# Loading two weight matrices in 32-row transfers, with a new order of the work

## The chip, the cores and the metric

One core of a Trainium2 chip runs the whole program. The metric is the device time of one execution in microseconds (us), median over several runs; less is better.

## The reference, cut to what matters

An RWKV-style recurrence over r, k, v of shape (4, 8, 768, 48) is followed by a feed-forward block on 3072 tokens of 384 columns:

```
cur = einsum('bhd,bhe->bhde', u * k_t, v_t)
y_t = einsum('bhd,bhde->bhe', r_t, state + cur)
state = w * state + einsum('bhd,bhe->bhde', k_t, v_t)
x = y as (3072, 384)
out = (((x @ w1) * (x @ w2)) @ w3) @ w_out
```

w1 and w2 are 384 x 1024, w3 is 1024 x 1024, w_out is 1024 x 384. These four arrive as 8-byte floats; everything is computed in 4-byte floats.

## The kernel before, in words

The sequence is cut into 24 units (six chunks of 128 steps for each of four batches). For a unit, k and r are scaled with tables of powers of w (`k`, line 432), turned so that head columns stand on partitions (`T`, `R` by PE for the first five units; `x`, `y`, `z`, `l` through a scratch in device memory for the others: VectorE turns blocks, SP writes them out and reads them back into the tile tt, ScalarE copies), multiplied (`U` line 551, `A` line 561, `S` line 670, `V` line 700), taken (`Y`), turned (`yt`) and put into xT (`yx`). Then come the products with w1 and w2 (`a`, `b`, line 748: full ones of 512 tokens, half ones of 256; for later chunks `pa`, `pb`, line 907, in halves of the width) and their elementwise product (`u`, `ga`, `gb`).

w3 and w_out don't depend on the tokens, so the kernel multiplies them once: w34 = w3 @ w_out, in eight folds (`F`, line 419, one for each block of 128 rows of w3; each needs all eight pieces of w_out, and its block of w3 turned by VectorE, `G`, line 412). The products with w34 are made by a scheme of seven products instead of eight (`s`, `P` line 807, `E`, `D`); those of `pa` and `pb` use the like for w1 and w2.

The weights come in 32 pieces (`W`, lines 233 to 244): eight strips of w1 and w2 (768 KB), eight pieces of w_out (384 KB), sixteen of w3 (512 KB; two for each fold). Each lands in one of three raw buffers, `raws[i % 3]`. The 8-byte floats are then made into 4-byte ones in five steps (lines 365 to 403): `M` magnitude (ScalarE), `p` sign (POOL, line 391; `N` is the same on VectorE, line 382), `H` high word (VectorE, line 395), `L` low word (ScalarE, line 398), `Q` total (VectorE, line 402). After `L` the raw buffer is free for the third piece on. The sign tile has two buffers.

At the start a table of powers is made (lines 281 to 306), turned by PE (line 311) and put into pn_in (line 313), with which k and r of the first units are scaled.

All engines but the two branches around it follow one list, ORDER (lines 23 to 104): each word is one step on its engine (`names`, line 957), each engine takes its instructions in the order of the list, and so do SP's transfers. A transfer that waits on SP holds all that come behind it. With 1425 words before and after, the list is where every step stands in its queue.

Of the kernel before, what the change touches and what calls it, by code (L numbers as in the profile page):

```python
# [28 lines left out]
V.3 Q.2 W.5 c.0.0.0 U.5 Y.3 H.4 ps p.3 v.6 M.3 cz.1 ub L.4 H.3 yt.3 W.7 b.0.0.0 Q.4 yx.3 L.3 k.7 a.0.2.2 W.6 Q.3 M.5
p.5 z.5 u.0.0.0 vs.6 u.0.1.0 H.5 a.0.4.2 c.0.2.2 e.5 L.5 f.5 Q.5 M.7 p.7 b.0.1.1 h.5 c.0.4.2 H.7 a.0.0.1 W.8 M.6 p.6  # L30
d.6 e.6 L.7 b.0.4.2 H.6 c.0.0.1 W.10 L.6 Q.7 Q.6 M.8 p.8 W.9 b.0.2.2 l.5 H.8 f.6 L.8 p.10 Q.8 M.10 W.11 H.10 b.0.5.2
u.0.2.2 M.9 p.9 u.0.4.2 L.10 H.9 W.13 Q.10 L.9 Q.9 a.0.1.1 M.11 p.11 W.12 d.7 H.11 kr.10 a.0.5.2 c.0.1.1 e.7 L.11 f.7
W.14 M.13 p.13 Q.11 H.13 M.12 p.12 u.0.1.1 b.0.3.2 L.13 H.12 c.0.5.2 W.16 Q.13 L.12 u.0.5.2 W.15 Q.12 a.0.6.2 M.14
p.14 d.8 e.8 H.14 L.14 p.16 M.16 Q.14 W.17 A.5 M.15 p.15 H.16 b.0.6.2 c.0.6.2 i.5 L.16 m.5 W.19 j.5 H.15 a.0.3.2 L.15
Q.16 M.17 Q.15 W.18 p.17 G.0.0 H.17 b.0.0.1 p.19 u.0.6.2 L.17 c.0.3.2 Q.17 W.20 a.0.7.2 G.0.1 M.18 p.18 u.0.3.2 M.19
u.0.0.1 H.18 F.0 H.19 L.18 L.19 Q.18 W.21 M.20 Q.19 p.20 W.22 c.0.7.2 G.1.0 G.1.1 H.20 L.20 p.21 M.21 Q.20 W.23 F.1
X.0 H.21 M.22 p.22 G.2.0 L.21 H.22 W.24 Q.21 L.22 Q.22 M.23 p.23 W.25 G.2.1 H.23 U.4 X.1 G.3.0 F.2 L.23 i.4 p.24 M.24
W.26 j.4 Q.23 M.25 G.3.1 p.25 k.6 x.6 kr.9 M.26 H.25 y.6 S.4 H.24 L.25 F.3 fe.4 L.24 Q.25 W.28 X.2 Q.24 p.26 G.4.0
W.27 H.26 G.4.1 L.26 x.7 z.6 Q.26 M.28 p.28 V.4 H.28 X.3 U.6 Y.4 v.7 p.27 S.5 cz.0 L.28 y.7 yt.4 fe.5 k.8 V.5 yx.4
W.29 F.4 M.27 Q.28 l.6 G.6.0 v.8 H.27 vs.7 Y.5 W.31 L.27 x.8 g.6 Q.27 z.7 p.29 M.29 f.8 P.0.0.0 H.29 X.4 vs.8 G.5.0  # L40
p.31 yt.5 y.8 L.29 A.6 G.5.1 W.30 yx.5 b.0.7.2 m.6 g.7 i.6 kr.11 j.6 Q.29 l.7 S.6 G.6.1 U.7 fe.6 z.8 u.0.7.2 A.7 M.30
p.30 V.6 m.7 M.31 F.6 i.7 j.7 v.9 H.30 Y.6 L.30 H.31 l.8 Q.30 G.7.0 L.31 s.0.1.0 vs.9 U.8 wa.0 A.8 X.6 wa.1 F.5 Q.31
G.7.1 wa.3 wb.0 wa.2 s.0.1.1 i.8 k.9 yt.6 X.5 F.7 wb.1 yx.6 g.8 wb.3 x.9 k.10 y.9 s.0.1.2 j.8 m.8 S.7 s.0.0.0 X.7 U.9
z.9 fe.7 B.0 V.7 P.0.1.0 Y.7 B.1 yt.7 v.10 E.0.1.0 s.0.0.1 pa.1.0.0 yx.7 xs.1.0 E.0.0.0 P.0.1.2 ga.1.0.0 xs.1.1 xs.1.2
xs.1.3 l.9 pb.1.0.4 B.3 pa.1.0.4 vs.10 x.10 pa.1.0.1 B.2 y.10 s.0.0.2 k.11 pa.1.0.5 ga.1.0.5 pb.1.0.0 s.0.1.3 ga.1.0.1
ga.1.0.3 pa.1.0.6 z.10 s.0.0.3 pa.1.0.7 ga.1.0.2 x.11 pa.1.0.3 ga.1.0.4 y.11 wb.2 d.9 pa.1.0.2 ga.1.0.7 e.9 kr.12
gb.1.0.0 f.9 d.10 g.9 pb.1.0.5 e.10 kr.13 f.10 pa.1.1.0 d.11 pb.1.0.1 e.11 gb.1.0.1 kr.14 f.11 ga.1.0.6 gb.1.0.3
pb.1.0.6 gb.1.0.5 pb.1.0.7 d.12 gb.1.0.2 e.12 pb.1.0.2 gb.1.0.4 gb.1.0.8 E.0.1.2 pb.1.0.3 gb.1.0.6 s.1.0.0 s.1.0.1 S.8
# [1035 lines left out]
```

## Time and profile before

| | |
|---|---|
| median of 3 runs | 564.42 us (563.61 to 565.67) |
| profiled execution | 559.54 us, span 557.8 us |
| busy | PE 493.7, PEld 402.7, VectorE (DVE) 328.5, ScalarE (ACT) 196.2, GpSimd (POOL) 64.9 us |
| moved by DMA | 52.72 MB, mean 95 GB/s |

PE is the matmul engine and PEld its weight loads. "SPq" is SyncE's queue, which issues the transfers. A matmul of 4-byte floats stands as two instructions in the trace, so a fold of eight matmuls is x16. "PEclk" is the granted clock as a share of the upper level. An engine's idle time matters only where others wait for it.

### The profile page before, as it was taken

Reading aid. Unit: us, or ns where it says so; the run is one execution under the profiler, and the core shown is the slowest. Engines: PE = TensorE matmul, PEld = TensorE weight load, DVE = VectorE, ACT = ScalarE, POOL = GpSimd, SP = SyncE. Lnnn points to the kernel's source line nnn. Section 1 sums busy time; section 2 is a strip of 40 time slices with the busy share of each in tenths; the row PEclk is TensorE's granted clock in tenths of the full one; section 3 lists DMA queues with packets and bytes.
Section 4 is the critical chain, followed back from the end, with each engine's and each line's share of the span. In section 5 each row is a group of like instructions: output and inputs, shape, how many; then the busy total and the mean of one; then the engine's idle time right before and its main releaser. Section 6 shows DMA issues by size and latency. Waiting matters only on the chain.

```text
span 557.8 us, 12087 instructions
## 1 busy us (share of the span) xinstructions
PE 493.7 (89%) x5084; PEld 402.7 (72%) x5084; DVE 328.5 (59%) x645; ACT 196.2 (35%) x450; POOL 64.9 (12%) x61
## 2 busy tenths in 40 slices
PE   7889674774547799999999999999999999999996
...
PEclk9989878687859799999999999999999999999999
DMA  8998232222344424403236326622220001000001
GB/s 183 224 242 241 103 101 100 100 97 101 122 140 146 115 72 117 98 15 114 59 106 138 86 73 176 153 58 86 72 86 29 29 28 43 31 31 0 1 0 63
DMA packets 99104, 52.72 MB, mean 95 GB/s; under 512 B 77920, under 2 KB 88416, under 8 KB 99040
## 3 DMA queue, kind: packets, MB, share of 16 engines
...
q8 instruction: 42, 0.69, 0.5%
...
q10 hardware_dynamic: 624, 0.00, 0.1%
...
## 4 chain that ended last, share of the span: by engine, by line
PE 66%; DMA 20%; DVE 4%; SPq 3%; ACT 3%; POOL 2%; issue 1%; ACTq 0%; POOLq 0%; DVEq 0%
DMA raw<-in_moe_w_dram 10%; PE ps_accB L917 9%; DMA raw<-in_moe_w_out_dram 5%; DMA tt<-scratch 5%; PE ps_Ab L917 3%; PE ps_accC L917 3%; PE ps_accC L921 3%; PE ps_accB L921 3%; PE ps_s4b L812 3%; PE ps_s3t L812 3%; PE ps_s1t L812 3%; PE ps_s2t L812 3%; PE ps_a22t L812 3%; PE ps_Aa L917 3%; PE ps_a12b L812 3%; PE ps_a11b L812 3%
## 5 line engine op out<-in xcount | busy, mean ns | idle before, releaser
L391 POOL TENSOR_SCALAR t<-raw 128x512 f32<-128x512 f32 (+2 forms) x32 | 54.5, 1705 | 121.1 <-DMA raw<-in_moe_w_dram 75.2
L422 PE MATMUL ps_w<-wo,w3T 128*128 128x384 f32 x128 | 48.9, 541 | 10.2 <-DVE w3T L417 10.2
L422 PEld LDWEIGHTS ps_w<-wo,w3T 128*128 128x128 f32 x128 | 26.6, 213 | 29.4 <-issue 12.9
L917 PE MATMUL ps_accB<-sumw,w 128*128 128x256 f32 x160 | 45.6, 387 | 0.0
L754 PE MATMUL ps_a<-xT,w 128*128 128x512 f32 (+1 forms) x60 | 29.8, 651 | 11.9 <-DVE abt L763 11.9
L396 DVE SCALAR_TENSOR_TENSOR w3n<-w3n,t 128x512 uint32<-128x512 uint32 x16 | 10.9, 691 | 44.4 <-POOL t L391 44.4
L466 ACT ACTIVATE ynat<-vnat,dg 128x48 f32<-128x48 f32 x144 | 34.4, 324 | 0.1
L522 ACT COPY kT<-tt 128x1024 f32<-128x1024 f32 x19 | 19.9, 1046 | 36.9 <-PE ps_y L685 31.8
L917 PEld LDWEIGHTS ps_accB<-sumw,w 128*128 128x128 f32 x160 | 28.9, 190 | 5.5 <-ACT u3a L934 1.1
L754 PEld LDWEIGHTS ps_a<-xT,w 128*128 128x128 f32 x60 | 13.8, 241 | 25.6 <-DVE abt L763 14.3
L754 PE MATMUL ps_b<-xT,w 128*128 128x512 f32 (+1 forms) x60 | 25.1, 567 | 7.9 <-ACT a L760 7.0
L400 ACT ACTIVATE t<-raw 128x512 uint32<-128x512 uint32 (+2 forms) x32 | 22.2, 701 | 22.9 <-DVE w3n L396 11.8
L436 DVE TENSOR_TENSOR krs<-krin,pn_in 128x768 f32<-128x768 f32 (+1 forms) x25 | 23.3, 937 | 9.5 <-PE ps_a L565 5.3
L380 ACT ACTIVATE w3n<-raw 128x512 f32<-128x512 f32 x16 | 10.4, 665 | 49.6 <-DMA raw<-in_moe_w_dram 49.6
L685 PE MATMUL ps_y<-st,kT 64*64 64x48 f32 x320 | 14.5, 226 | 13.0 <-ACT w L425 11.9
L754 PEld LDWEIGHTS ps_b<-xT,w 128*128 128x128 f32 x60 | 12.4, 217 | 18.1 <-ACT a L760 8.1
L685 PEld LDWEIGHTS ps_y<-st,kT 64*64 64x64 f32 x320 | 11.8, 138 | 18.4 <-ACT w L425 12.2
L917 PE MATMUL ps_accC<-xT,sumw 128*128 128x256 f32 x80 | 24.1, 383 | 0.1
L921 PE MATMUL ps_accB<-xT,w 128*128 128x256 f32 x80 | 23.8, 379 | 0.0
L921 PE MATMUL ps_accC<-xT,w 128*128 128x256 f32 x80 | 23.8, 379 | 0.0
L917 PE MATMUL ps_Ab<-xT,w 128*128 128x256 f32 x80 | 22.7, 385 | 0.3 <-DVE ynat L717 0.3
L730 ACT COPY xT<-ps_x 128x384 f32<-128x384 f32 x24 | 11.4, 482 | 32.0 <-PE ps_x L724 31.9
...
## 6 DMA issues: line engine op xcount, KB each, us to landing
...
```

The lines of the kernel that those rows point to most:

```text
L391: nc.gpsimd.tensor_scalar(part["t", i].bitcast(F32), words(i)[1].bitcast(F32), 0.0, None, ALU.mult)
L400: nc.scalar.activation(out=part["t", i], in_=words(i)[0], func=COPY, scale=2.0 ** -29)
L422: nc.tensor.matmul(ps, lhsT=w3T[j][:, kc, :], rhs=wo[kc], start=(kc == 0), stop=(kc == KF - 1))
L436: nc.vector.tensor_mul(krs[n % NS][:, which, :, :D], kr[:, which], pn[:, which, :, :D])
L466: nc.scalar.activation(out=ynat[n][:, h, :], in_=vnat[n % NV][:, h, :], func=COPY, scale=dg[n][:, h:h + 1])
L522: nc.scalar.copy(out=turned(n).rearrange("x g p (z t) -> x (g p) z t", t=Q), in_=tts.rearrange("x z e t -> x e z t"))
L685: nc.tensor.matmul(yt[n][i][rows(a), p, :], lhsT=rw[rows(i), p, rows(a)], rhs=(half[n % 2] if a else st[b][(c + 1) % 2])[rows(i), p, :], s ...
L730: nc.scalar.copy(out=xT[c][:, :, b * C:(b + 1) * C], in_=pst["y", n])
L754: nc.tensor.matmul(ps, lhsT=(w1 if x == "a" else w2)[:, z, q, js], rhs=xT[c][:, q, ts], start=(q == 0), stop=(q == KM - 1))
L812: nc.tensor.matmul(ps, lhsT=operand(c, j // 2, a)[:, j % 2, m * C:(m + 1) * C], rhs=w34[:, KH * (x == 1) + j, :DH] if x < 2 else made[b][: ...
L917: nc.tensor.matmul(ps, lhsT=quarter(w, g, i, x), rhs=(b11, b21, b22, t4, b12, t2, t3)[x], start=x in (0, 4) and i == 0, stop=True, skip_gr ...
L921: nc.tensor.matmul(ps, lhsT=wide_of[w][:, g + half * HZ, 2, i * P:(i + 1) * P], rhs=xT[c][:, 2, side * TH:(side + 1) * TH], start=False, s ...
```

## The change

Three edits in the code and a new list.

1. `fetch`: a piece of w_out was one transfer with four blocks of rows outermost (4 x 32 x 384 elements), a piece of w3 two such (4 x 32 x 256). Now each piece is four transfers, one for each block of 32 partitions, with the 32 rows outermost.
2. The power tables: PE multiplied the 64-column table twice, once for each half of the partitions. Now the 64 columns are copied beside themselves, one table by VectorE and one by ScalarE, and PE turns 128 columns at once. Both takes are on ScalarE.
3. In the list the signs of pieces 0 and 1 are `N` (VectorE) instead of `p` (POOL), the odd values of unit 0 are taken by ScalarE (`vs.0` for `vp.0`), and two single idle matmuls `Z.1.1` become `Z.4.0` and `Z.3.0`. All other words are the same, in a new order.

```
@@ fetch
-            if i < NAB + KF:
-                queue.dma_start(out=landed[i] if i < NAB else landed[i][:, 0], in_=pieces[i])
-            else:
-                j, z = divmod(i - NAB - KF, NW3)
-                for f in range(2):
-                    queue.dma_start(out=landed[i][:, 0, f * DF // NBLOCK:(f + 1) * DF // NBLOCK],
-                                    in_=moe_w3[j * P:(j + 1) * P].rearrange("(f r) (q x) -> f q r x", r=Q, q=NBLOCK)[2 * z + f])
+            if i < NAB:
+                queue.dma_start(out=landed[i], in_=pieces[i])
+                return
+            j, z = divmod(i - NAB - KF, NW3)
+            for q in range(NBLOCK):
+                to = landed[i][q * Q:(q + 1) * Q, 0]
+                if j < 0:
+                    queue.dma_start(out=to, in_=pieces[i][q])
+                else:
+                    queue.dma_start(out=to.rearrange("r (f x) -> r f x", f=2),
+                                    in_=moe_w3[j * P:(j + 1) * P].rearrange("(f r) (q x) -> q r f x", r=Q, q=NBLOCK)[q, :, 2 * z:2 * z + 2])
@@ power tables
+        nc.vector.tensor_copy(out=both[:, 0, :, T:], in_=both[:, 0, :, :T])
+        nc.scalar.copy(out=both[:, 1, :, T:], in_=both[:, 1, :, :T])
             for p in range(NP):
-                for a in range(2):
-                    nc.tensor.matmul(ps[rows(a), p, :], lhsT=both[:, g, p, :T], rhs=ident, start=True, stop=True)
-            put = nc.vector.tensor_copy if g else nc.scalar.copy
-            put(out=pn_in[:, g].rearrange("t h d -> t (h d)"), in_=ps.rearrange("x p t -> x (p t)"))
+                nc.tensor.transpose(ps[:, p, :], both[:, g, p, :], ident)
+            nc.scalar.copy(out=pn_in[:, g].rearrange("t h d -> t (h d)"), in_=ps.rearrange("x p t -> x (p t)"))
```

From the new list, its first line and the lines from the first piece of w_out (`W.8`) to the last fold (`F.7`):

```
v.1 kr.2 uw k.1 vs.0 ka.0 Z.4.0 T.1 kb.0 T.0 t.1 v.2 U.0 N.0 t.0 R.0 kr.3 ku.0 i.0 j.0 vp.1 U.1 R.1 i.1 r.0 j.1 r.1
...
W.7 cz.1 a.0.3.2 L.5 Q.4 W.8 M.6 Q.5 p.6 c.0.0.1 vs.6 k.6 b.0.2.2 c.0.3.2 z.5 x.6 H.6 u.0.1.0 M.7 p.7 b.0.4.2 e.5 f.5
M.8 y.6 h.5 kr.7 L.6 j.4 H.7 S.4 W.9 U.5 L.7 fe.4 Q.6 V.4 l.5 Q.7 p.8 W.10 cz.0 Y.4 A.5 H.8 a.0.2.2 m.5 L.8 W.11 i.5
j.5 M.9 p.9 Q.8 b.0.3.2 k.7 c.0.2.2 z.6 H.9 M.10 p.10 u.0.2.2 L.9 Q.9 a.0.4.2 H.10 u.0.3.2 L.10 W.12 p.11 M.11 Q.10
x.7 a.0.1.1 c.0.4.2 H.11 W.13 L.11 u.0.4.2 U.6 l.6 Q.11 a.0.6.2 k.8 W.14 c.0.1.1 d.6 M.12 p.12 e.6 f.6 v.7 H.12
b.0.0.1 y.7 c.0.6.2 d.7 kr.9 p.13 M.13 e.7 L.12 b.0.1.1 f.7 H.13 Q.12 A.6 M.14 u.0.0.1 p.14 b.0.6.2 L.13 W.15 i.6 vs.7
Q.13 H.14 j.6 L.14 W.16 Q.14 a.0.5.2 u.0.6.2 m.6 W.17 x.8 M.15 p.15 u.0.1.1 a.0.7.2 c.0.5.2 d.8 e.8 z.7 H.15 M.16 p.16
b.0.5.2 L.15 c.0.7.2 Q.15 H.16 W.18 M.17 p.17 L.16 yt.4 Q.16 S.5 yx.4 U.7 g.6 fe.5 W.19 H.17 V.5 b.0.7.2 G.0.0 Y.5
L.17 v.8 u.0.5.2 W.20 l.7 Q.17 p.18 G.0.1 yt.5 M.18 A.7 u.0.7.2 g.7 F.0 i.7 y.8 kr.10 p.19 H.18 j.7 M.19 m.7 L.18 H.19
yx.5 W.21 M.20 Q.18 G.1.0 L.19 p.20 Q.19 vs.8 W.22 U.8 G.1.1 X.0 S.6 H.20 F.1 k.9 L.20 z.8 Q.20 G.2.0 M.21 p.21 x.9
fe.6 H.21 W.23 M.22 p.22 k.10 L.21 V.6 Q.21 X.1 S.7 H.22 W.24 l.8 fe.7 G.2.1 V.7 L.22 Y.7 A.8 W.25 Q.22 yt.7 F.2 G.3.0
yx.7 M.23 p.23 Y.6 i.8 y.9 v.9 j.8 kr.11 M.24 p.24 H.23 m.8 L.23 Q.23 M.25 G.3.1 p.25 yt.6 W.26 X.2 pa.1.0.0 H.24 yx.6
f.8 L.24 F.3 H.25 ga.1.0.0 Q.24 L.25 W.27 Q.25 g.8 G.4.0 G.4.1 W.28 vs.9 x.10 p.26 M.26 d.9 F.4 z.9 e.9 X.3 f.9 H.26
M.27 p.27 d.10 L.26 e.10 g.9 Q.26 H.27 W.29 p.28 G.5.0 f.10 L.27 Q.27 P.0.0.0 M.28 W.30 X.4 G.5.1 l.9 P.0.1.0 H.28
d.11 L.28 y.10 F.5 e.11 W.31 Q.28 M.29 p.29 G.6.0 f.11 kr.12 H.29 M.30 p.30 v.10 L.29 Q.29 H.30 pa.1.0.1 z.10 X.5
G.6.1 p.31 L.30 M.31 Q.30 F.6 ga.1.0.5 G.7.0 xs.1.0 E.0.0.0 xs.1.1 xs.1.2 kr.13 vs.10 H.31 s.0.1.0 L.31 Q.31 s.0.1.1
xs.1.3 U.9 wa.0 X.6 A.9 wa.1 pa.1.0.4 wa.2 pa.1.0.5 G.7.1 wa.3 F.7 ga.1.0.1 wb.0 ga.1.0.3 wb.2 k.11 s.0.1.2 kr.14 i.9
...
```

Between `W.8` and `F.7` stand, before and after:

| words | before | after |
|---|---|---|
| F; G; X | 8; 16; 7 | 8; 16; 7 |
| a, b full; half | 10; 2 | 11; 3 |
| P; pa of one width; pa doubled (x 1 to 3) | 1; 0; 0 | 2; 3; 1 |
| U, A, S, V, yt | 4, 4, 3, 3, 3 | 5, 5, 4, 4, 4 |
| k, x, m, d, e, f | 3, 3, 3, 3, 3, 3 | 5, 5, 4, 6, 7, 7 |
| kr, v, y, z between W.8 and W.31 | 2, 2, 2, 1 | 4, 3, 5, 5 |

## Rows read from the trace of the kernel before

**Rows 1.** The page: busy time, and its 40 slices of 13.9 us each

```profile
PE 493.7 (89%) x5084; PEld 402.7 (72%) x5084; DVE 328.5 (59%) x645; ACT 196.2 (35%) x450; POOL 64.9 (12%) x61
...
PE   7889674774547799999999999999999999999996
...
PEclk9989878687859799999999999999999999999999
...
DMA  8998232222344424403236326622220001000001
```

**Rows 2.** Windows: length, busy us of PE, PEld, DVE, ACT, POOL; PEclk, DMA share, GB/s

```profile
0.00:52.80 52.80, 45.57 (x840) 35.59 (x840) 38.41 (x85) 29.02 (x63) 26.98 (x36) 0.97 0.93 231
40.50:52.80 12.30, 12.30 (x104) 7.37 (x102) 10.63 (x15) 7.36 (x14) 8.15 (x4) 1.00 1.00 290
52.80:205.00 152.20, 101.68 (x670) 56.58 (x673) 78.75 (x138) 51.53 (x105) 37.87 (x25) 0.80 0.33 107
205.00:557.80 352.80, 346.48 (x3579) 310.53 (x3579) 211.34 (x425) 115.63 (x283) 0.00 (x0) 1.00 0.25 69
```

**Rows 3.** Timeline of SP at 50 and PE at 199 us: start, us

```profile
52.77 6.87 SPq L239 DMA_DIRECT2D raw<-in_moe_w_out_dram  x3
...
199.66 5.33 PE L422 MATMUL ps_w<-wo,w3T 128*128 128x384 f32 x16
```

**Rows 4.** Chain of waits, 30 to 200 us: start, us, what

```profile
47.34 6.67 DMA raw<-in_moe_w_dram
...
90.65 10.92 DMA raw<-in_moe_w_dram
...
101.71 1.53 POOL t L391
...
103.27 0.70 DVE w3n L396
...
103.99 0.67 ACT t L400
...
120.78 12.28 DMA raw<-in_moe_w_dram
```

**Rows 5.** Timeline of POOL, 100 to 120 us

```profile
106.92 1.51 POOL L391 TENSOR_SCALAR t<-raw 128x512 f32<-128x512 f32 x1 [3.69 <-DMA raw<-in_moe_w_dram]
```

**Rows 6.** DMA view, 90 to 140 us: totals, SP's queue (packets, MB, share)

```profile
DMA packets 2442, 5.00 MB, mean 100 GB/s; under 512 B 74, under 2 KB 74, under 8 KB 2440
...
q1 hardware_dynamic: 2440, 4.98, 25.9%
```

**Rows 7.** Chain of waits at 189 and 342 us: the reload of tt

```profile
188.96 2.96 DMA tt<-scratch
...
342.45 3.66 DMA tt<-scratch
```

**Rows 8.** Lines 518 and 239, issues: ns min/median/max, first, last start

```profile
L518 SPq DMA_DIRECT2D tt<-scratch x76: 313/424/3413, 47.8 to 465.5; - x76
...
L239 SPq DMA_DIRECT2D raw<-in_moe_w_out_dram x8: 532/532/3594, 52.8 to 83.3; - x8
```

**Rows 9.** Chain of waits, whole span: PE's prices

```profile
33.93 2.56 PE ps_b L754 x6
...
194.14 5.36 PE ps_w L422 x16
...
243.48 1.30 PE ps_s4b L812 x8
...
244.78 0.86 PE ps_Fb L917 x4
```

**Rows 10.** Timeline of DVE and POOL, 9 to 12 us; line 396 by form

```profile
9.18 0.69 DVE L313 COPY pn_in<-ps_p 128x512 f32<-128x512 f32 x1 [2.19 <-PE ps_p L311]
...
11.63 2.20 POOL L391 TENSOR_SCALAR t<-raw 128x768 f32<-128x768 f32 x1 [4.27 <-DMA raw<-in_moe_w_dram]
...
L396 DVE SCALAR_TENSOR_TENSOR w<-w,t 128x768 uint32<-128x768 uint32 x8 | 8.2, 1023 | 1.9 <-POOL t L391 1.9
```

More of the change, by code (lines that the diff above doesn't have):

```diff
@@ L29 @@
[L29 to L48, printed above, removed]
@@ new lines @@
+A.0 kr.4 Au.0 k.2 M.0 S.1 S.0 ku.1 m.0 vp.2 R.2 T.2 mo.0 W.1 t.2 H.0 A.1 W.2 r.2 Au.1 fe.0 k.3 L.0 V.0 kr.5 Y.0 m.1
+R.3 T.3 ku.2 mo.1 U.2 Q.0 A.2 t.3 Au.2 i.2 r.3 v.3 m.2 yt.0 M.1 mo.2 yx.0 fe.1 ku.3 k.4 Z.3.0 A.3 W.3 V.1 p.2 N.1 R.4
+Y.1 v.4 H.1 T.4 M.2 S.2 j.2 kr.6 yt.1 L.1 Au.3 fe.2 H.2 V.2 yx.1 vp.3 Y.2 m.3 a.0.0.0 mo.3 L.2 W.4 yt.2 Q.1 M.3 U.3
+W.5 i.3 p.3 t.4 Q.2 b.0.0.0 r.4 v.5 yx.2 k.5 ku.4 a.0.1.0 ub x.5 vp.4 c.0.0.0 A.4 H.3 c.0.1.0 S.3 y.5 ps fe.3 M.4 p.4
+u.0.0.0 j.3 L.3 d.5 V.3 W.6 Q.3 M.5 U.4 v.6 Au.4 H.4 p.5 Y.3 kr.8 m.4 yt.3 L.4 b.0.1.0 mo.4 yx.3 i.4 vp.5 a.0.0.1 H.5
@@ new lines @@
+pb.1.0.2 gb.1.0.4 gb.1.0.8 pa.1.1.6 gb.1.0.6 pb.1.1.0 ga.1.1.3 ga.1.1.2 s.1.0.0 pa.1.1.7 s.1.0.1 P.0.1.1 ga.1.1.4
+s.1.0.3 pb.1.1.4 s.1.0.2 E.0.1.1 pa.1.1.2 P.0.0.4 ga.1.1.6 pa.1.1.3 E.0.0.4 E.0.0.5 D.0.0.0 S.8 ga.1.1.7 U.10 gb.1.1.0
+fe.8 V.8 k.12 l.10 pb.1.1.5 v.11 x.12 z.11 A.10 gb.1.1.1 Y.8 pb.1.1.1 gb.1.1.3 i.10 m.10 pb.1.1.2 y.12 vs.11 kr.15
+gb.1.1.5 j.10 P.1.0.0 gb.1.1.6 yt.8 E.1.0.0 P.0.1.5 yx.8 g.10 U.11 P.0.1.6 k.13 f.12 P.1.1.0 d.13 e.13 kr.16 x.13
+pb.1.1.7 E.1.1.0 P.0.1.3 y.13 pb.1.1.6 E.0.1.3 E.0.1.6 E.0.1.7 P.0.1.4 gb.1.1.2 D.0.1.1 gb.1.1.4 pb.1.1.3 gb.1.1.8
@@ new lines @@
+s.1.1.0 s.1.1.1 P.1.0.5 gb.1.1.7 s.1.1.3 P.1.0.2 s.1.1.2 E.0.1.4 E.1.0.2 P.1.0.6 E.0.1.5 D.0.1.0 P.1.0.3 P.1.1.2
+E.1.0.3 E.1.0.6 P.1.0.1 E.1.1.2 P.1.0.4 E.1.0.1 E.1.0.7 D.1.0.1 P.1.1.1 E.1.0.4 E.1.0.5 D.1.0.0 P.1.1.3 E.1.1.1 S.9
+E.1.1.3 P.1.1.5 fe.9 l.11 z.12 V.9 E.1.1.6 A.11 Y.9 P.1.1.4 i.11 j.11 v.12 yt.9 m.11 P.1.1.6 yx.9 E.1.1.4 g.11 E.1.1.5
+D.1.1.0 S.11 E.1.1.7 S.10 D.1.1.1 fe.11 V.11 fe.10 l.12 f.13 V.10 v.14 Y.11 U.12 v.13 vs.12 k.14 A.12 z.13 yt.11
+pa.2.0.0 m.12 yx.11 Y.10 ga.2.0.0 i.12 yt.10 vs.14 pa.2.0.1 j.12 yx.10 x.14 g.12 U.13 xs.2.0 y.14 xs.2.1 S.12 xs.2.2
@@ new lines @@
+pa.2.0.4 xs.2.3 ga.2.0.5 fe.12 d.14 g.13 pa.2.0.5 e.14 kr.17 f.14 pa.2.1.4 d.15 e.15 V.12 ga.2.0.1 f.15 vs.13 pa.2.0.6
+v.15 Y.12 l.13 ga.2.0.3 yt.12 pb.2.0.0 d.16 ga.2.0.2 e.16 z.14 pa.2.0.7 yx.12 k.15 g.14 pa.2.0.3 ga.2.0.4 x.15 kr.18
+pa.2.0.2 ga.2.0.7 f.16 y.15 d.17 gb.2.0.0 e.17 vs.15 pb.2.0.5 ga.2.0.6 gb.2.0.1 pb.2.0.1 l.14 pb.2.0.6 gb.2.0.5 z.15
+pb.2.0.4 gb.2.0.2 A.13 gb.2.0.3 pb.2.1.4 i.13 m.13 pb.2.0.7 j.13 pa.2.1.0 gb.2.0.4 U.14 gb.2.0.8 A.14 k.16 pb.2.0.3
+i.14 kr.19 j.14 pb.2.0.2 gb.2.0.7 m.14 ga.2.1.0 x.16 pa.2.1.1 gb.2.0.6 y.16 s.2.0.0 pa.2.1.5 ga.2.1.5 s.2.0.1 pb.2.1.0
@@ new lines @@
+s.2.0.3 ga.2.1.1 ga.2.1.3 pa.2.1.6 s.2.0.2 pa.2.1.2 ga.2.1.2 pa.2.1.7 ga.2.1.6 pa.2.1.3 ga.2.1.4 S.13 ga.2.1.7 U.15
+gb.2.1.0 fe.13 V.13 k.17 l.15 pb.2.1.1 v.16 Y.13 z.16 x.17 yt.13 gb.2.1.5 pb.2.1.5 yx.13 g.15 P.2.1.0 y.17 kr.20
+P.2.0.0 gb.2.1.1 f.17 vs.16 gb.2.1.3 pb.2.1.6 d.18 E.2.1.0 E.2.0.0 S.14 e.18 gb.2.1.2 A.15 fe.14 l.16 pb.2.1.3 i.15
+j.15 z.17 m.15 V.14 gb.2.1.7 U.16 Y.14 P.2.1.1 v.17 k.18 x.18 kr.21 S.15 A.16 fe.15 E.2.1.1 y.18 pb.2.1.7 l.17 m.16
+i.16 yt.14 vs.17 pb.2.1.2 j.16 yx.14 gb.2.1.4 g.16 gb.2.1.8 S.16 gb.2.1.6 U.17 fe.16 V.15 s.2.1.0 z.18 V.16 Y.15 A.17
@@ new lines @@
+Y.16 yt.15 m.17 yt.16 yx.15 pa.3.0.0 xs.3.0 g.17 v.18 xs.3.1 v.19 P.2.0.1 s.2.1.1 xs.3.2 i.17 pa.3.0.4 ga.3.0.0 j.17
+l.18 pa.3.0.5 s.2.1.3 ga.3.0.1 pa.3.0.1 xs.3.3 s.2.1.2 vs.18 ga.3.0.3 yx.16 pa.3.0.6 k.19 ga.3.0.5 vs.19 pb.3.0.0 x.19
+ga.3.0.2 pa.3.0.7 f.18 y.19 d.19 g.18 P.2.1.2 ga.3.0.4 kr.22 e.19 P.2.1.6 f.19 d.20 e.20 pa.3.0.3 z.19 f.20 d.21 e.21
+pa.3.0.2 E.2.1.2 ga.3.0.7 E.2.0.1 gb.3.0.0 pb.3.0.1 ga.3.0.6 pb.3.0.4 gb.3.0.5 pa.3.1.4 P.2.1.3 pb.3.0.5 E.2.1.3
+pa.3.1.0 gb.3.0.1 pb.3.0.6 gb.3.0.3 pb.3.0.7 gb.3.0.2 pb.3.0.3 gb.3.0.4 gb.3.0.8 pb.3.0.2 gb.3.0.7 ga.3.1.0 pa.3.1.5
@@ new lines @@
+gb.3.0.6 pa.3.1.1 s.3.0.0 ga.3.1.1 ga.3.1.3 s.3.0.1 pa.3.1.7 ga.3.1.5 s.3.0.3 pa.3.1.2 s.3.0.2 pa.3.1.6 ga.3.1.6 S.17
+ga.3.1.2 U.18 fe.17 l.19 ga.3.1.4 V.17 A.18 Y.17 v.20 P.2.0.2 m.18 k.20 yt.17 P.2.1.5 x.20 kr.23 yx.17 g.19 i.18 y.20
+pa.3.1.3 j.18 E.2.0.2 f.21 vs.20 P.2.0.3 d.22 ga.3.1.7 e.22 E.2.1.6 P.2.0.4 E.2.0.3 E.2.1.7 D.2.1.1 P.2.0.5 z.20
+pb.3.1.0 E.2.0.6 U.19 gb.3.1.0 E.2.0.4 A.19 k.21 pb.3.1.5 i.19 P.2.0.6 gb.3.1.1 j.19 m.19 pb.3.1.1 x.21 E.2.0.7 y.21
+E.2.0.5 U.20 D.2.0.0 gb.3.1.5 S.18 D.2.0.1 pb.3.1.6 fe.18 l.20 k.22 V.18 gb.3.1.2 A.20 Y.18 v.21 P.3.1.0 z.21 m.20
@@ new lines @@
+i.20 pb.3.1.4 x.22 E.3.1.0 P.3.0.0 gb.3.1.3 y.22 vs.21 pb.3.1.7 E.3.0.0 pb.3.1.2 gb.3.1.4 gb.3.1.8 P.3.0.4 gb.3.1.6
+s.3.1.0 P.2.1.4 s.3.1.1 s.3.1.2 P.3.0.5 E.2.1.4 E.2.1.5 D.2.1.0 P.3.0.2 P.3.1.2 E.3.0.2 P.3.0.3 E.3.1.2 P.3.1.3
+E.3.0.3 E.3.0.6 E.3.0.4 E.3.0.5 P.3.1.4 E.3.1.3 D.3.0.0 yt.18 E.3.1.4 P.3.1.5 yx.18 g.20 S.19 E.3.1.6 E.3.1.5 pb.3.1.3
+fe.19 D.3.1.0 l.21 f.22 d.23 gb.3.1.7 V.19 z.22 S.20 s.3.1.3 U.21 A.21 fe.20 Y.19 V.20 i.21 P.3.0.6 v.22 Y.20 v.23
+m.21 yt.20 P.3.1.1 e.23 yx.20 k.23 l.22 P.3.1.6 x.23 g.22 E.3.1.1 y.23 yt.19 E.3.1.7 pa.4.0.0 D.3.1.1 U.22 ga.4.0.0
```

83 lines of the change are left out of this document (23 added, 60 removed).

## The prediction

> **What bounds the kernel now.** I read the page's busy shares and slices first: PE is busy 89% of the span, but its slices fall to 4 to 7 tenths between the fourth and the fourteenth, just where the DMA row drops from 9 tenths to 2 and where the granted clock is lowest [rows 1]. So the kernel has one loose stretch, early, and a tight rest. The windows put numbers on it [rows 2]. Until 52.8 us the DMA engines are 0.93 busy at 231 GB/s. From 52.80 to 205.00 us, 152.2 us, PE is busy 101.68 us at a granted clock of 0.80 of its upper level (2.4 GHz), and the DMA share is 0.33. From 205.00 to the end PE is busy 346.48 of 352.80 us at clock 1.00: nothing but PE's own list matters there.
>
> What starts and ends the loose stretch: at 52.77 us SP issues the first piece of w_out (W.8), and at 204.99 us PE ends the last of the eight folds (F.7), which needs the last piece of w3 [rows 3]. The chain of waits shows what fills it: one lap after another of a transfer into a raw buffer, POOL's sign (1.53), VectorE's high word (0.70), ScalarE's low word (0.67), after which that buffer is fetched into again [rows 4]. Two laps lie between the transfers that start at 90.65 and 120.78 us, 15.07 us each, and three buffers share them: a w3 piece of 512 KB about every 5.2 us, as POOL's starts say (101.71, then 106.92) [rows 4, 5]. Transfers, not work, are most of a lap: 10.92 to 12.28 us [rows 4].
>
> The DMA view of 90 to 140 us shows the cause: 100 GB/s and a share of 25.9%, level, with up to three pieces waiting [rows 6]. A share that stands at a quarter while work is queued is four engines of sixteen; just before, with w1 and w2 pieces in flight, the share was 1.00 and the rate 290 GB/s [rows 2]. The loads named in the diff have four blocks of rows as their outermost dimension.
>
> **The loads.** The change issues each piece as four transfers, one for each block of 32 partitions, with the rows outermost. No row shows this shape from these matrices. The nearest is the reload of tt from scratch, also four transfers with at most 32 partitions outermost, 384 KB in all: it lands 2.96 to 3.66 us after its last issue [rows 7]. A dearer bound is the 768 KB piece on full queues, 6.67 us [rows 4]. The DMA page of the Trainium skill ("DMA: Bandwidth & Descriptors", why a DMA increments its semaphore by 16) says that a transfer runs on the largest number of engines up to 16 that divides the outermost sizes: 4 before, 16 after; by that alone a piece of 512 KB would take 1.9 us of the engines and not 5.2.
>
> An issue takes SP a median of 0.424 us in that shape and 0.53 in the old ones, at worst 3.4 to 3.6 where SP is held [rows 8]. A lap becomes: three issues ahead of the last one, 4 x 0.424 to 4 x 0.53 = 1.7 to 2.1; landing 2.96 to 6.67; POOL, VectorE and ScalarE 2.9 as now; some 0.2 of hand-over. That is 7.8 to 11.9 us, and 24 pieces on three buffers are eight laps: 62 to 95 us where the loose stretch has 152.2. By bytes: 24 pieces are 11.5 MB, and the new list puts four kr, three v and five each of scratch writes and reloads between W.8 and W.31, 6.1 MB more; 17.6 MB at the 290 and 231 GB/s of [rows 2] is 61 to 76 us. By SP: 96 issues of weights and some 40 others at 0.424 to 0.53 are 58 to 72 us. None of the three reaches what the engines have to do, so the transfers stop being the bound. What is late next is the work itself.
>
> **PE's work up to F.7, in the new list.** Prices [rows 9]: a fold 5.36, a full product of a or b 2.56 (a half 1.28), a product of the seven 1.30, a half-width product 0.86. Before, between W.8 and F.7: eight folds 42.9, ten full and two half products 28.2, one of the seven 1.3, and the units' small matmuls, 9.0 by the same kind of counting: 81.4. After: eight folds 42.9, eleven full and three half 32.0, two of the seven 2.6, three half-width products at 0.86 and one doubled 4.3, five groups more of units' matmuls, 11.7 in all: 93.5 us. Ahead of W.8 the new list has 3.3 us less (one full and five halves instead of two and six, the rest small). So behind F.7 about 8.5 us less is left: 352.8 - 8.5 = 344.3 us, since PE is tight there.
>
> **VectorE's work.** It is busy 78.75 of the 152.2 us [rows 2]; the new list has 26 more of its instructions there (scalings, block turns, r.k sums, takes). At the 0.70 of [rows 4], above their mean, that is 18, so 97 us. It is as near to the bound as PE. POOL (37.87) and ScalarE (51.53 and twelve more) are not.
>
> So the stretch cannot take less than about 97 us: 93.5 / 0.98 = 95, at the share that PE reaches behind F.7 (346.48 of 352.80), or VectorE's 97. Upward the nearest row is the stretch ahead of W.8, where transfers run on all engines and converting, products and units are mixed in the same way: PE was busy 45.57 of 52.80 us there, 0.863, with VectorE at 0.73, and at 0.86 in the last 12.3 us of it [rows 2]. I take PE's 0.863: 93.5 / 0.863 = 108 us; the bounds are 97 us and what VectorE's shares give in rival (1). The granted clock should stand nearer to its upper level than the 0.80 of now: ahead of W.8 it was 0.97, behind F.7 1.00 [rows 2].
>
> **The head.** Two signs of 768 columns move from POOL (2.20 us each) to VectorE, where no row has the operation; the nearest is its high word, 1.02, so 2.0 us on VectorE for 4.4 on POOL [rows 10]. The turned tables lose half of their matmuls and gain two copies; both takes are now on ScalarE, which frees VectorE from the 0.69 take that ended at 9.87 [rows 10]: between 0.7 earlier and 0.7 later for the first scaled k. All of it lies beside DMA engines that are 0.93 busy; were that cover gone, it would be worth under 2 us. The list has one kr load and one reload less ahead of W.8, 0.8 MB, 3 us at 231 GB/s. I put W.8 at 50 us (47 to 53).
>
> **Sum.** 50 + 108 + 344 = 502 us of span. The profiled execution took 559.54 for a span of 557.8, and the median of the runs is 564.42, 4.9 more: 502 + 1.7 + 4.9 = 508.6 us.
>
> **Rivals.** (1) *VectorE in its order decides.* Each step of a weight waits for POOL or ScalarE in turn. If VectorE passes its 97 us at 0.77, between its 0.73 and 0.86 ahead of W.8 [rows 2] and nearer to the first, that is 126 us: 50 + 126 + 344 + 6.6 = 527. For it: VectorE is at 0.52 now, and each fold needs two turns on it. Chance 0.25. (2) *PE is fed all the time*: 97 us, 498 us in all. For it: the list has products ready; against it, in-order engines. Chance 0.12. (3) *The transfers stay on four engines*: 5.2 us a piece as now, the stretch stays at 152, only the 8.5 us of moved work and W.8's 3 us are gained: 553. Against it: the reload [rows 7]. Chance 0.03. (4) *Slower: the issues on SP decide.* Each transfer holds the queue as a full one does, 136 issues in a row, kr loads and reloads behind them. It ties at 152 / 136 = 1.1 us an issue; at 1.2 they take 163, and 12 more pass until the last piece has landed (3), is converted and turned (4) and its fold is done (5.4): 50 + 175 + 344 + 6.6 = 576. For it: the worst issues, 3.4 and 3.6 us [rows 8]; against it, the median, and four transfers that land in 2.96 us together [rows 7]. Chance 0.04. The same page has a rule that speaks for this one ("Anatomy of one DMA": about 2.0 us fixed for each transfer; "Rules for kernel authors": parts of the partitions serialize, one transfer for all 128 is advised); were the fixed parts added, 96 transfers of up to 128 KB would be up to 96 x 2.3 = 221 us, an estimate from that page, and the kernel slower; the reload's row disagrees, as its four fixed parts overlap.
>
> **How the numbers follow.** The forecast, 508.6, has 0.56, with a range of its own of 499 to 520 (stretch 99 to 119). Rivals (1) and (2) lie at 527 and 498; a range of 493 to 530 holds the forecast and most of both; left out are the best of (2), the worst of (1), and (3) and (4). A measurement of this kernel tells 0.5% from no change. Faster by more: 0.95; within: 0.01; slower: 0.04.
>
> **What would show it.** The share of DMA in what is now 52.8 to 205 above 0.5 and rates of 150 GB/s or more; a w3 piece each 3 to 4.5 us at POOL; F.7 ending near 158 us; waits of POOL and ScalarE for raw transfers a third of now; PE's clock 0.9 or more there; from F.7 to the end 344 us. A DMA share that stays at a quarter, SP issues of over 1 us, or a PE that waits for VectorE's turns and multiplies would prove me wrong, in this order of rivals (3), (4), (1).

## The result, and the profile after

The changed kernel takes 499.1 us (median of 4 runs, 498.07 to 500.03); the kernel before, run beside it, 564.01 (563.48 to 565.67). The ratio is 0.8844, 95% interval 0.8816 to 0.8872: 11.6% faster. 508.6 was forecast, 493 to 530 the range.

The page after: busy shares and the 40 slices, now of 12.4 us each.

```profile
PE 474.9 (96%) x5070; PEld 395.7 (80%) x5070; DVE 329.5 (66%) x647; ACT 198.0 (40%) x454; POOL 65.5 (13%) x57
...
PE   8698899989999999999999999999999999999994
...
PEclk9998999999999999999999999999999999999998
DMA  8988968989931004326524550144240000000002
```

PE's hole between the fourth and the fourteenth slice [rows 1] is gone, and so is the low clock there. The DMA row stays at 8 and 9 (once 6) for eleven slices and has then little left to do, where it stood at 2 to 4 for ten [rows 1].

The same three windows as in [rows 2], cut at the new W.8 and the new end of F.7 (length, busy us of PE, PEld, DVE, ACT, POOL; clock, DMA share, GB/s):

```profile
0.00:48.20 48.20, 39.64 (x806) 34.39 (x807) 36.63 (x85) 29.70 (x64) 21.07 (x31) 0.93 0.86 219
48.20:148.70 100.50, 97.68 (x847) 59.05 (x846) 93.05 (x161) 58.60 (x124) 44.47 (x27) 1.00 0.82 203
148.70:496.30 347.60, 337.61 (x3421) 302.21 (x3419) 199.83 (x402) 109.72 (x267) 0.00 (x0) 0.99 0.23 63
```

Most of the gain, 51.7 of 61.5 us of span, is in the second line: 100.50 us for 152.20, with more work in it (PE 847 instructions for 670, VectorE 161 for 138). PE is busy 0.97 of it and VectorE 0.93, at a granted clock of 1.00 for 0.80, and the DMA engines carry 203 GB/s for 107. The part behind it is 5.2 us shorter, the head 4.6.

The issues of w_out (line 245) and w3 (line 247) on SP, with the landing times of w3; then the end of F.7 on PE's timeline:

```profile
L245 SPq DMA_DIRECT2D raw<-in_moe_w_out_dram x32: 311/419/1508, 48.2 to 78.0; - x32
L247 SPq DMA_DIRECT2D raw<-in_moe_w_dram x64: 311/425/1312, 78.5 to 130.0; - x64
...
DMA to landing us min/median/max: 2.5/3.6/5.1
```

```profile
143.35 5.37 PE L427 MATMUL ps_w<-wo,w3T 128*128 128x384 f32 x16
```

The 24 pieces go out from 48.2 to 130.0 us, 3.4 us apart. Before, w3's were 5.2 apart in the laps that the prediction read, and 6.4 over all sixteen (issued from 81.8 to 178.3 us). An issue takes a median of 0.42 us, as the reload's row said [rows 8], and a transfer lands in 3.6, within the two bounds that were taken from [rows 4, 7]. The issues of w3 before (line 243):

```profile
L243 SPq DMA_DIRECT2D raw<-in_moe_w_dram x32: 531/532/3374, 81.8 to 178.3; - x32
```

Waits for the pieces, first after (48 to 149 us), then before (53 to 205 us): total, times, longest.

```profile
POOL t L396 <- DMA raw<-in_moe_w_dram: 15.1, 7, 3.9
...
ACT w3n L385 <- DMA raw<-in_moe_w_dram: 6.6, 7, 2.1
```

```profile
POOL t L391 <- DMA raw<-in_moe_w_dram: 62.7, 15, 6.5
ACT w3n L380 <- DMA raw<-in_moe_w_dram: 49.6, 14, 6.9
```

The chain of waits after, where it passes from pieces to folds:

```profile
92.36 3.62 DMA raw<-in_moe_w_dram
...
100.53 3.47 DMA raw<-in_moe_w_dram
...
109.18 5.16 PE ps_w L427 x16
...
115.53 10.32 PE ps_w L427 x32
125.85 2.60 PE ps_a11b L817 x16
128.45 5.16 PE ps_w L427 x16
```

A transfer is still on the chain, but for 3.5 to 3.6 us where it was 10.9 to 12.3 [rows 4]; from 109 us on the chain is PE's own work, fold after fold.

### The profile page after: what moved, and what is told of

It is laid out like the page before. It is cut to its first block, busy times and chain, and to the rows that moved or that the text cites. A ratio compares the mean times of both kernels' runs of the same rounds, so it can differ in the third digit from the quotient of the medians.

```text
span 496.3 us, 12176 instructions
## 1 busy us (share of the span) xinstructions
PE 474.9 (96%) x5070; PEld 395.7 (80%) x5070; DVE 329.5 (66%) x647; ACT 198.0 (40%) x454; POOL 65.5 (13%) x57
## 4 chain that ended last, share of the span: by engine, by line
PE 78%; DVE 7%; ACT 4%; DMA 3%; issue 2%; POOL 1%; SPq 1%; ACTq 0%; DVEq 0%; POOLq 0%
PE ps_accB L922 10%; PE ps_w L427 6%; PE ps_Ab L922 4%; PE ps_accC L926 3%; PE ps_accC L922 3%; PE ps_accB L926 3%; PE ps_Aa L922 3%; PE ps_s4b L817 3%; PE ps_a12b L817 3%; PE ps_a11b L817 3%; PE ps_s3t L817 3%; PE ps_s1t L817 3%; PE ps_a22t L817 3%; PE ps_s2t L817 3%; DMA raw<-in_moe_w_dram 3%; PE ps_a L759 2%
## 5 line engine op out<-in xcount | busy, mean ns | idle before, releaser
L427 PE MATMUL ps_w<-wo,w3T 128*128 128x384 f32 x128 | 42.7, 488 | 0.1
L427 PEld LDWEIGHTS ps_w<-wo,w3T 128*128 128x128 f32 x128 | 24.0, 190 | 15.6 <-issue 0.4
L759 PE MATMUL ps_b<-xT,w 128*128 128x512 f32 (+1 forms) x60 | 23.6, 538 | 0.5 <-DVE half L609 0.5
L922 PE MATMUL ps_Aa<-xT,w 128*128 128x256 f32 x80 | 22.3, 382 | 0.4 <-ACT ps_accB L937 0.4
L759 PE MATMUL ps_a<-xT,w 128*128 128x512 f32 (+1 forms) x60 | 22.2, 515 | 0.0
L922 PE MATMUL ps_accB<-sumw,sumw 128*128 128x256 f32 x80 | 20.7, 382 | 0.0
L621 DVE COPY_PREDICATED AT<-later,ps_a 128x512 f32<-128x512 int32 x24 | 17.6, 731 | 1.8 <-PE ps_a L591 1.4
L570 PE MATMUL ps_a<-kT 64*64 64x64 f32 x768 | 17.2, 226 | 1.5 <-ACT kT L527 0.9
L511 DVE STREAM_TRANSPOSE tr<-krs 128x768 f32<-128x768 f32 x19 | 18.4, 969 | 0.2
```

The lines of the kernel that those rows point to most:

```text
L427: nc.tensor.matmul(ps, lhsT=w3T[j][:, kc, :], rhs=wo[kc], start=(kc == 0), stop=(kc == KF - 1))
L511: nc.vector.transpose(out=blocks[n].rearrange("x m e t -> x e m t"), in_=krs[n % NS][:, :, :, :D])
L621: nc.vector.copy_predicated(AT[n], later.bitcast(I32)[:, None, None, :].to_broadcast([C, 2, NP, T]), upper(n))
L759: nc.tensor.matmul(ps, lhsT=(w1 if x == "a" else w2)[:, z, q, js], rhs=xT[c][:, q, ts], start=(q == 0), stop=(q == KM - 1))
L922: nc.tensor.matmul(ps, lhsT=quarter(w, g, i, x), rhs=(b11, b21, b22, t4, b12, t2, t3)[x], start=x in (0, 4) and i == 0, stop=True, skip_gr ...
```

## The experiments

In the short diffs, "-" is the changed kernel unless said otherwise. Every ratio is against the kernel before, run on the same chip.

**The loads alone.** The kernel before, with the new `fetch` and nothing else.

```
  (list and head of before)
+            for q in range(NBLOCK):
+                to = landed[i][q * Q:(q + 1) * Q, 0]
...
```

> The kernel before with the new loads alone: old list, old head. Theory A (the engines that a transfer runs on are the whole matter): the stretch from W.8 to F.7 shrinks to PE's 81.4 us of listed work at 0.86 to 0.97, 84 to 95 us, and 352.8 us follow as before: 52 + 84 to 95 + 353 = 489 to 500 us of span, the changed kernel's 496.3 within 1.5%. Theory B (the new list is needed to use the faster pieces, since the old one keeps steps waiting in the places that slow pieces gave them): the stretch stays above 105 us and the span above 510. In both the DMA share of the stretch rises above 0.6.

503.86 us, ratio 0.8992 (0.8935 to 0.9048). Windows, cut at its W.8 and F.7:

```profile
53.30:148.10 94.80, 85.67 (x677) 48.34 (x677) 81.60 (x140) 51.35 (x107) 41.11 (x26) 0.98 0.68 174
148.10:500.30 352.20, 346.19 (x3579) 310.15 (x3579) 210.82 (x424) 115.50 (x283) 0.00 (x0) 1.00 0.26 69
```

Theory A: a list made for slow pieces uses the fast ones well enough. The stretch is 94.8 us, at the upper end of what was expected. Its 81.4 us of listed PE work go through at 81.4 / 94.8 = 0.86. F.7 ends at 148.1 us here and at 148.7 in the changed kernel, whose list has W.8 5.1 us sooner and 12.1 us more of PE's work between the two: the changed kernel's lead of 4.0 us of span shows only behind F.7 (347.6 us for 352.2), less 0.6 us at F.7.

**The list alone.** The changed kernel with the old `fetch`.

> The changed kernel with the old loads: new list, new head. Both theories: w3 pieces stay 5.2 us apart, the DMA share of the stretch near 0.35 and the stretch near 150 us; span 48 + 150 + 347 = 545 us, 3% faster than before by the moved work (8.5 us) and the earlier W.8 (3 to 5 us). If the list by itself does something for the loads, it is under 535.

555.41 us, ratio 0.9891 (0.9853 to 0.993).

```profile
46.90:208.40 161.50, 114.29 (x842) 66.52 (x840) 91.99 (x163) 57.58 (x125) 40.21 (x27) 0.83 0.42 126
```

Faster by 1.1%, not by 3: the stretch grew to 161.5 us, 9 more than with the old list. More work was listed into it behind pieces that come as slowly as before (w3's are issued over 92 us for 96); that this work made the 9 us is likely and was not tested. Loads alone give 10.1%, the list alone 1.1, both 11.6.

**As many transfers, cut the other way.** Four for each piece, by columns; each has all 128 partitions and four blocks of rows outermost, as before.

```
-                    queue.dma_start(out=to, in_=pieces[i][q])
+                    queue.dma_start(out=landed[i][:, 0, cs], in_=pieces[i][:, :, cs])
...
+                    queue.dma_start(out=landed[i][:, 0, 2 * P * f + P * c:2 * P * f + P * (c + 1)],
+                                    in_=moe_w3[j * P:(j + 1) * P].rearrange("(f r) (q x) -> f q r x", r=Q, q=NBLOCK)[2 * z + f, :, :, xs])
```

> The changed kernel with as many transfers (four for each piece) but cut by columns, all 128 partitions each, four blocks of rows outermost as before. If the outermost size decides the engines: pieces stay 5 us apart, DMA share of the stretch 0.25 to 0.4, time within 2% of the run with the old loads (about 547 us). If more and smaller transfers in flight are what helps: near the changed kernel, 499 us. Runs are half as long (1 KB and 768 B), which may cost some per cent of the transfers' time.

566.25 us, ratio 1.0092 (1.0062 to 1.0122). The window of the stretch, and the DMA view of 100 to 180 us:

```profile
45.80:214.70 168.90, 115.64 (x841) 66.29 (x841) 91.81 (x162) 57.26 (x125) 40.22 (x27) 0.84 0.42 120
```

```profile
GB/s 96 198 109 95 88 96 96 110 154 87 87 285 171 116 52 91 69 96 169 122 96 87 104 89 96 96 96 119 294 151 93 134 78 94 95 96 96 96 185 106
```

With the same list, the same number of transfers and the same bytes, the rate stands at 96 GB/s wherever only weights are in flight, and the time is 67 us longer. It isn't the number or size of transfers that helps, but the outermost dimension. Nor is it the 32 partitions of a transfer: the strips of w1 and w2, each one transfer of 128 partitions with its rows outermost, were in flight when the share stood at 1.00 [rows 2]. (This cut costs 11 us more than the old loads under the same list, and runs at 96 GB/s where those had 102; whether the shorter runs or the larger number of issues cost it was not separated.) This is the rule on the number of engines that the prediction drew from the Trainium skill ("DMA: Bandwidth & Descriptors", "Why a DMA increments its semaphore by 16 and not by 1"). The measurements agree with it: a share of 0.26 with four blocks outermost [rows 6], 0.82 over the new stretch with 32 rows. No row counts the engines of a transfer; four of sixteen is read from the share.

**Twice as many transfers.** Eight of 16 partitions each.

```
-            for q in range(NBLOCK):
+            for q, h in ((q, h) for q in range(NBLOCK) for h in range(2)):
+                hs = slice(h * Q // 2, (h + 1) * Q // 2)
```

> The changed kernel with each piece as eight transfers of 16 partitions. 96 more issues at 0.42 us are 40 us of SP. If PE is the bound of the stretch and SP has room: 499 us, within 1%. If the issues on SP are as near to the bound as the rival on SP said: 10 to 40 us more, and issues longer than 0.42 us would not show but SP without pauses would.

531.74 us, ratio 0.9469 (0.9434 to 0.9504): 32 us more. The window of its stretch, the issues of w3, and a stretch of SP's timeline:

```profile
47.90:184.20 136.30, 108.52 (x841) 63.28 (x840) 91.83 (x162) 57.46 (x124) 41.38 (x27) 0.90 0.56 148
```

```profile
L248 SPq DMA_DIRECT2D raw<-in_moe_w_dram x128: 311/422/1642, 90.4 to 167.1; - x128
```

```profile
101.08 7.58 SPq L248 DMA_DIRECT2D raw<-in_moe_w_dram  x16
108.76 0.38 SPq L218 DMA_DIRECT2D vnat<-in_v_dram  x1
109.24 4.97 SPq L248 DMA_DIRECT2D raw<-in_moe_w_dram  x8
114.31 0.37 SPq L516 DMA_DIRECT2D scratch<-tr  x1
```

An issue takes a median of 0.42 us here with 64 KB as in the changed kernel with 96 and 128 KB, and SP has hardly a pause: from 47.87 to 167.99 us its timeline's rows add up to 117.4 of 120.1 us. So SP's queue is the likely bound here: 96 issues more at 0.42 us are 40 us, and 32 came. It is SP that rival (4) named, but by the number of issues and not by their length, and the kernel is still faster than before. Counted in the same way SP is taken 76 of 82 us in the changed kernel: there is room for the four, and hardly for one more.

**Half of the folds' matmuls.** Which engine bounds the new stretch? PE is busy 0.97, so taking 21 us from PE should show it. Every second matmul of the folds is left out, so w34 is incomplete.

```
-            for kc in range(KF):
+            for kc in range(0, KF, 2):
```

> The changed kernel with every second matmul of the eight folds left out (32 of 64; the product w3 w_out is then incomplete). They are 8 x 2.6 = 21 us of PE in the stretch. If PE bounds it: 18 to 21 us less, 478 to 481 us. If VectorE, the transfers or SP bound it: under 8 us less, above 491.

499.23 us, ratio 0.8872 (0.8846 to 0.8898): nothing gained. Windows of its stretch, then of its two halves (cut at the first fold); in the second fence the two halves of the changed kernel's stretch:

```profile
47.30:149.30 102.00, 84.15 (x777) 49.83 (x776) 91.59 (x158) 57.68 (x124) 44.05 (x27) 0.92 0.82 197
...
47.30:94.90 47.60, 44.11 (x415) 23.77 (x413) 41.24 (x71) 25.75 (x54) 22.31 (x15) 0.93 0.76 202
94.90:149.30 54.40, 40.04 (x367) 26.06 (x364) 50.35 (x88) 31.93 (x72) 21.73 (x13) 0.91 0.88 193
```

```profile
48.20:92.80 44.60, 43.12 (x420) 23.54 (x418) 40.70 (x70) 25.78 (x54) 22.39 (x14) 1.00 0.84 214
92.80:148.70 55.90, 54.56 (x435) 35.52 (x428) 52.36 (x92) 32.82 (x72) 22.08 (x13) 1.00 0.81 193
```

In the first half there are no folds: nothing was taken away there, and PE is busy 0.93. In the second PE idles 14 of 54 us, and the folds still end at 149 us. The pieces kept their pace: the last was issued at 131.9 us, 1.9 later. So a PE that is busy 0.97 does not show that PE is what the time hangs on; in the second half something else would have ended the stretch at the same place. For the first half that is not shown: its PE work, mostly the products of a and b, was taken away in no run.

**No high-word step for w3.** VectorE is next (0.93). The step is left out for the 16 pieces of w3.

```
         def high(i):
+            if i >= NAB + KF:
+                return
```

> The changed kernel without the high-word step of the 16 pieces of w3 (their values are then not those of the input). 16 x 0.69 = 11 us less on VectorE in the stretch, and a shorter lap from landing to a free buffer. If VectorE or the laps bound the stretch: 6 to 11 us less, 488 to 493. If PE does: within 2 us of 499.

497.11 us, ratio 0.8835 (0.8811 to 0.8859), the same as the changed kernel. The window says that VectorE lost the work and nobody gained by it:

```profile
48.50:148.70 100.20, 96.25 (x841) 58.02 (x840) 84.14 (x146) 58.29 (x125) 43.40 (x27) 1.00 0.84 203
```

**Both left out**, the folds' matmuls and the high word.

> Half folds and no high-word step for w3 (both left out of the computation): 21 us less of PE and 11 less of VectorE. Theory V (each of the two engines held the stretch when the other was relieved): 485 to 490. Theories S and B: 496 to 499, as with either alone.

498.56 us, ratio 0.8886 (0.8849 to 0.8924). Not that either: with PE at 82.3 and VectorE at 80.9 of 99.5 us the stretch is as long as ever.

```profile
47.10:146.60 99.50, 82.32 (x776) 49.44 (x775) 80.87 (x141) 56.60 (x124) 41.13 (x27) 0.93 0.83 202
```

The end of its chain of waits shows the kind of thing that holds it:

```profile
131.79 4.73 DMA vnat<-in_v_dram
...
136.54 0.35 ACT vodd L699
...
136.90 0.35 ACT vodd L699
...
137.27 0.69 ACT t L407
...
137.99 0.69 DVE w3n L410
```

In the list `vs.10` stands ahead of `L.31` on ScalarE. It waits for v of unit 10, which SP issues behind the last pieces of w3; so the last piece's low word, its total and the last fold wait for a load of another unit. Earlier in the same chain PE's products of a and b stand one behind the other, from 59 to 93 us:

```profile
74.21 2.59 PE ps_b L761 x12
...
80.20 5.15 PE ps_a L761 x12
85.35 2.58 PE ps_b L761 x6
```

**Two queues.** ScalarE issues two of each piece's four transfers.

```
             for q in range(NBLOCK):
+                queue = nc.sync if q < 2 else nc.scalar
```

> The changed kernel with two of the four transfers of each piece of w_out and w3 issued by ScalarE (48 of 96, some 20 us of ScalarE's queue, which is 0.58 busy). If SP's issues set the pace of the pieces, the last piece is issued 10 us or more earlier than the 130 us of now, and the time falls to what PE's 97.7 busy us of the stretch allow: 2 to 4 us less, 495 to 497. If they do not: the last issue stays at 130, and ScalarE's issues cost 0 to 6 us: 499 to 505.

499.35 us, ratio 0.8903 (0.8873 to 0.8933): no gain, at best the same. ScalarE has 48 issues more in its order, and the last piece is issued at 132 us and not earlier:

```profile
L248 SPq DMA_DIRECT2D raw<-in_moe_w_dram x32: 311/317/1583, 78.8 to 132.1; - x32
L248 ACTq DMA_DIRECT2D raw<-in_moe_w_dram x32: 318/373/656, 80.6 to 132.2; - x32
```

**Two queues and half the folds.**

> The same with every second matmul of the folds left out as well (w3 w_out incomplete), so that PE no longer hides the pace. Theory S (SP's issues): last piece issued 10 us or more before 130, time 480 to 490. Theory B (bytes in flight) and theory V (VectorE's order): as the half folds alone, 499 within 3 us.

498.38 us, ratio 0.8875 (0.8839 to 0.891). SP's issues alone don't set the pace of the changed kernel, although SP is taken nine tenths of the time: with half of them on ScalarE and PE relieved too, the pieces come no sooner. What may, is said by the heads of two chains of waits from 93 to 149 us (shares of that time), first of this run, then of the run without half of the folds and the high word:

```profile
by line: DVE w3n L409 13.2%; DVE w3n L402 12.0%; issue 11.6%; DVE w3T L423 10.0%; ACT t L406 7.2%; DMA raw<-in_moe_w_dram 5.4%; PE ps_w L428 5.1%; DVE ruk L454 3.6%; DVE ruk L451 3.3%; ACT ynat L472 3.1%; DVE krs L442 3.1%; PE ps_accB L923 
```

```profile
by line: PE ps_w L429 13.8%; DMA raw<-in_moe_w_dram 12.1%; ACT t L407 8.7%; DMA vnat<-in_v_dram 8.4%; SPq L247 8.0%; DMA tt<-scratch 6.4%; ACT ynat L473 6.1%; ACT w3n L385 4.7%; PE ps_accB L924 4.6%; issue 4.6%; ACT vodd L699 2.5%; DVE w3n 
```

Added up by engine, the chain of the changed kernel is on PE for 41 of these 56 us. With half of the folds out and half of the pieces' issues on ScalarE, it is on VectorE for 33. With half of the folds and VectorE's high word out, VectorE has 4 left, and transfers and ScalarE have 15 each.

**Half the bytes and half the folds.** Each transfer carries half the columns; the rest of the buffer keeps what lay there.

```
-                    queue.dma_start(out=to, in_=pieces[i][q])
+                    queue.dma_start(out=to[:, :DM // 2], in_=pieces[i][q][:, :DM // 2])
...
+                    queue.dma_start(out=to.rearrange("r (f x) -> r f x", f=2)[:, :, :P],
```

> Half folds, and each of the four transfers moves only half of the columns of each row (the other half is what lay in the buffer; values not those of the input). As many issues, half the bytes (5.8 MB less). Theory B: the pace quickens, last piece well before 122, time 480 to 490. Theories S and V: 499 within 4 us.

497.95 us, ratio 0.8878 (0.8843 to 0.8913). The transfers of w3 land in a median of 2.1 us for 3.6, the DMA share falls to 0.57, and the stretch stays:

```profile
46.00:146.80 100.80, 83.84 (x776) 49.32 (x775) 91.59 (x159) 56.92 (x124) 42.12 (x27) 0.92 0.57 143
```

Its waits in 46 to 147 us have changed their name: POOL now waits most for VectorE to give back one of the two sign tiles, and the chain of 93 to 149 us is on VectorE for 30 us.

```profile
POOL t L396 <- DVE w3n L408: 19.0, 9, 3.5
```

**The head, undone in two parts.** The old turning of the power tables (`both[:, g, p, :T]` multiplied twice, one take on VectorE), and the first two signs on POOL (`p.0`, `p.1` for `N.0`, `N.1` in the list).

> The changed kernel with the power tables turned as before (twice as many matmuls, one take on VectorE). The head lies beside full transfers: within 1 us of 499. If the first scaled k sets the pace of the head: 0.5 to 1 us more.

> The changed kernel with the first two signs on POOL again. POOL takes 2.2 us for each where VectorE took 0.55. If the transfers set the head: within 1 us of 499. If the conversion of the first pieces holds the third and fourth: 1 to 4 us more.

Old turning: 497.81 us, ratio 0.8843 (0.8819 to 0.8868), no difference. Signs on POOL: 500.3 us, ratio 0.8894 (0.8863 to 0.8924); its interval overlaps the changed kernel's (up to 0.8872) by a hair, so 0 to 1% may be there. Its head, up to the first piece of w_out, is 50.8 us for 48.2:

```profile
0.00:50.80 50.80, 42.70 (x812) 35.81 (x813) 34.75 (x82) 29.10 (x64) 25.27 (x33) 0.90 0.82 208
```

## Why the prediction was right, point by point

**The bound and its cause: right, and shown.** The loose stretch was lost to transfers that kept the DMA engines at a quarter of their share; the loads alone bring 10.1 of the 11.6%, and four transfers that keep the four blocks outermost bring nothing.

**The transfers' new cost: right.** Landing 3.6 us between the bounds of 2.96 and 6.67; an issue 0.42 us; 203 GB/s. That they "stop being the bound" holds for the bytes: half of them, with half of the folds out, changed nothing. The 1.9 us for a piece "by that alone" do not come out (a quarter of 5.2 is 1.3, and 512 KB at the 290 GB/s of [rows 2] take 1.8); nothing hung on them.

**SP: right in the sum, too sure in words.** The 58 to 72 us were 76. The rival on SP was put down for issues that get longer; they don't, but their number has its price at once: 96 more cost 32 us. The fixed 2.0 us that the prediction cites beside it from the Trainium skill ("DMA: Bandwidth & Descriptors", "Anatomy of one DMA") are given there for transfers that GpSimd issues. These are issued by SP, and pieces of four transfers went out every 3.4 us, 0.85 us for each transfer: no 2.0 us added up.

**The stretch: forecast 108 us, measured 100.5.** This is the step that was mis-sized, by 7.5 us, and its form was wrong too. The share of 0.863, at which PE's listed work would go through, was PE's mean over the whole head, slow start included (0.7 in the first slice [rows 1]); in the last 12.3 us of that head PE was busy all the time, 12.30 us [rows 2]. That the old list reaches 0.86 with the new loads bears the share out for that list alone; the new list reaches 93.5 / 100.5 = 0.93. And PE's listed work does not say when the stretch ends. F.7 ends at 148.1 us with 81.4 us of it (the loads alone), at 148.7 with 93.5, and at 149.3 with 21 us of folds taken out again. That the forecast of the whole came within 2% is in part luck. PE's clock came as forecast, 1.00; F.7 ended at 148.7 us for the 158 put down as a sign.

**What is late next: half right.** PE (0.97 busy) and VectorE (0.93; 93.05 us for the 97 forecast) did become the fullest engines, and the time came out where rival (2), with its chance of 0.12, had it: 498 us, "PE is fed all the time". But its reason does not stand alone: 21 us less of PE, 11 less of VectorE, both, half of SP's issues, or half the bytes beside half the folds gave 0 to 2 us. The chains say where the second half goes when PE is relieved: to VectorE in its order (with half the folds alone, to VectorE and the transfers), and when VectorE is relieved too, to transfers and ScalarE, the v load ahead of the last piece's low word among them. So at least two chains of about the same length seem to lie beside PE's there. No run relieved PE, VectorE and the transfers together, and none relieved PE's products of the first half; a third sign tile and a list made anew were not tried either. Which of these is the next bound stays open.

**Head: W.8 at 48.2 for 50 (47 to 53).** The first scaled k starts at 9.29 us for 10.11, and the signs take VectorE 0.55 and 0.71 us for the 1.02 allowed. Beside transfers that are 0.86 busy the new turning is worth nothing that its undoing shows; the signs may be worth a little.

**Behind F.7: 347.6 us for 344.3.** PE's busy time there fell by 8.9 us (337.61 for 346.48), as the moved work should (12.1 less 3.3 is 8.8; the prediction wrote 8.5). The length fell by 5.2 alone. 2.5 us of the difference of 3.3 lie after the last store: it was issued at 489.33 and the span ends at 496.3, 6.6 us after that issue's end, where it was 4.2 us before.

```profile
489.33 0.34 SPq L855 DMA_DIRECT2D out_dram<-osb_top  x1
```

```profile
553.32 0.33 SPq L850 DMA_DIRECT2D out_dram<-osb_top  x1
```

No engine works there, and among the other kernels it is 4.1 to 6.3 us without a pattern that the list or the loads explain; it stays open.

**The sum.** 502.3 us of span were forecast and 496.3 came: -1.8 (W.8), -7.5 (the stretch), +3.3 (behind F.7). Another 3.8 us were the step from the profiled execution to the median: 4.9 us before, 1.0 after (498.07 to 499.1). The profiled execution was the fastest of the four, so this is scatter of executions: beside the experiments the kernel before ran from 558.02 to 564.08 us.
